# One core: the parts of the first MLP product gathered in three PSUM banks instead of seven

## The chip, the cores and the metric

The kernel runs on one core of a Trainium2 chip. The metric is the device time of one execution in microseconds (us). Three executions of the kernel before took 1241.55, 1241.81 and 1246.07 us; the median is 1241.81 us.

## The reference

A block of 2 x 3008 tokens of width 256 goes through a Fourier transform along the sequence, a complex mixing of the channels with a soft threshold, and the inverse transform. The 6016 tokens that result go through two gated MLPs, one after the other:

```
h = x @ w_in            # 6016 x 256 times 256 x 2048
g = h * sigmoid(1.702 * h)   # in the second MLP: sigmoid(h)
x = g @ w_out           # 6016 x 2048 times 2048 x 256
```

The weights arrive in float64, and the kernel converts them to float32 on the chip.

## The kernel before

The program has four parts: the forward transform, the mixing, the inverse transform, and the two MLPs (layers 0 and 1). The change touches the MLPs alone.

The MLPs run over blocks of 1024 tokens, cut in two halves of 512 (the last block of a layer has halves of 448). Within a block they run over eight pairs of blocks of the inner width, so that there are 2 x 6 x 8 = 96 groups; `group` (L760) issues one. A group multiplies a 2 x 2 matrix of weight blocks with a 2 x 2 matrix of token blocks by the Strassen-Winograd scheme, with seven products in place of eight. `prod` (L767) makes one product of three matmuls (high part of the weights with the high and the low part of the tokens, then the low part of the weights with the high part of the tokens), and each product has a PSUM bank of its own, out of four (`ps0`). The four results are sums of the seven products:

```
h(0,0) = p1 + p2
h(0,1) = p1 + p6 + p5 + p3
h(1,0) = p1 + p6 + p7 + p4
h(1,1) = p1 + p6 + p7 + p5
```

The kernel before forms them in SBUF: ScalarE copies p1 (L794), and VectorE makes seven additions (`add`, L784), each of an SBUF tile and a product in PSUM. The tiles are the columns of `yt` that the block itself came from; `order` turns them by one step from group to group.

`gate` (L775) then applies the activation on ScalarE (L776, in place), copies the result to its high part on ScalarE (L778), and subtracts for the low part (L780; mostly on GpSimd, at some places on VectorE). `out_next` issues the second product of an earlier gate: six matmuls (L744), which add up over the whole block in four other banks (`ps1`). When a block is done, VectorE and ScalarE copy the four banks to `yt` (L748).

`hook` hangs other work between the steps: the splits of the next block's seven token factors in a high part (ScalarE, L99) and a low part (L100), the sums for them (L684 to L697), and the conversion of the weights: a DMA of float64 words (L146), one ScalarE instruction (L155), five on VectorE for a block of weights (L160 to L164), an addition (L221), a store (L224). In layer 0's last block the weights of layer 1 are loaded and put in place (L195 to L200, L99, L100). `add` also pumps the VectorE steps that wait in the list `fill`: the list `left` says among how many additions they are spread.

What sets the order: the program is written once, and a scheduler lays out each engine's queue. In some parts the order of the program is kept for VectorE and SyncE (`rest0`, `last0`: VectorE and SyncE; `rest1`, `last1`: VectorE). Each engine runs its own queue in order, and an instruction waits until what it reads is there and what it overwrites has been read; a product's first matmul waits for the last reader of its bank.

## Time and profile before

| | us |
|---|---|
| median of three runs | 1241.81 |
| span of the profiled execution | 1241.9 |
| TensorE matmuls, busy | 1193.9 (96%) |
| VectorE, busy | 904.3 (73%) |
| ScalarE, busy | 709.1 (57%) |
| GpSimd, busy | 691.3 (56%) |
| the additions L784, busy | 450.9 in 672 instructions |
| TensorE idle before the products L772 | 15.2 |

The page lists no time for the profiled execution beside its span; the span is 0.1 us from the median of the runs, so that time and span can be taken as the same here. The MLPs' first matmul starts at 216.4 us, so that they are some 1025 us of the span. Busy times of engines overlap and don't add up to the span. A matmul's duration in the profile (some 394 ns for 512 columns) overlaps with the next one's; the distance from one to the next is what a stretch's length gives when it is divided by their number.

### The profile page before, as it was taken

To read this page: it belongs to the slowest core of one execution; us is meant where nothing else is said; L and a number is where in the kernel's file an instruction comes from. 1 tells how busy PE (TensorE), PEld (TensorE's weight loads), DVE (VectorE), ACT (ScalarE), POOL (GpSimd) and SP (SyncE) were. 2 spreads that over 40 slices of the span, in tenths; PEclk is the share of its full clock that TensorE was granted. 3 is DMA by queue.
4 is the path that set the end of the run, shared out by engine and by line. 5 is a ranking of instruction groups with operands and counts; after the bars stand their busy time and mean duration, and the time that the engine had idled before them with its cause. 6 is when DMAs were issued, how large, how long until landed. Compare 5 with 4: busy or idle time off the path is not lost.

```text
span 1241.9 us, 15776 instructions
## 1 busy us (share of the span) xinstructions
PE 1193.9 (96%) x5220; PEld 969.5 (78%) x5220; DVE 904.3 (73%) x1543; ACT 709.1 (57%) x1393; POOL 691.3 (56%) x579
## 2 busy tenths in 40 slices
PE   7889889799999999999999999999999999999998
PEld 4877679577688787787888977888888888888897
DVE  7899999999967868678758886465564564655654
ACT  3566644656655656556556675565564555554654
POOL 4666655646545647547556575464464554553643
PEclk9889889799999999999999999999999999999999
DMA  8441123111110111111100110000000000000000
GB/s 330 170 160 55 52 73 130 36 52 60 33 44 27 39 39 39 39 39 38 43 18 9 56 39 9 1 35 1 1 34 1 1 35 1 27 8 1 35 1 30
DMA packets 33012, 57.11 MB, mean 46 GB/s; under 512 B 3233, under 2 KB 22689, under 8 KB 31650
## 3 DMA queue, kind: packets, MB, share of 16 engines
q1 hardware_dynamic: 30882, 41.42, 10.3%
q0 software_dynamic: 2048, 14.68, 3.2%
q8 instruction: 41, 0.67, 0.2%
q14 instruction: 41, 0.34, 0.1%
HBM read 44.68 MB, written 11.40 MB: 45 GB/s over the span
## 4 chain that ended last, share of the span: by engine, by line
PE 65%; DVE 7%; issue 2%; ACT 1%; POOL 0%; DMA 0%; DVEq 0%; ACTq 0%
PE o L744 35%; PE x L772 30%; DVE yt L784 3%; DVE cv_s L196 1%; DVE tmp L697 1%; DVE g L780 0%; DVE x L100 0%; ACT yt L776 0%; DMA raw<-in_wo 0%; DVE tmp L691 0%; ACT g L778 0%; ACT wi L99 0%; DVE cv_c L164 0%; ACT x L99 0%; DVE wi L100 0%
## 5 line engine op out<-in xcount | busy, mean ns | idle before, releaser
L784 DVE TENSOR_TENSOR yt<-yt,x 128x512 f32<-128x512 f32 (+1 forms) x672 | 450.9, 673 | 275.2 <-PE x L772 204.8
L780 POOL TENSOR_TENSOR g<-yt,g 128x512 fp32r<-128x512 f32 (+1 forms) x324 | 416.4, 1295 | 418.1 <-ACT g L778 301.2
L744 PE MATMUL o<-g,wo 128*128 128x512 f32 (+1 forms) x2304 | 604.3, 392 | 2.4 <-ACT yt L748 1.1
L772 PE MATMUL x<-x,wi 128*128 128x512 f32 (+1 forms) x2016 | 543.3, 394 | 15.2 <-DVE yt L784 10.8
L744 PEld LDWEIGHTS o<-g,wo 128*128 128x128 f32 x2304 | 432.9, 188 | 101.7 <-ACT g L778 2.8
L772 PEld LDWEIGHTS x<-x,wi 128*128 128x128 f32 x2016 | 378.4, 189 | 108.3 <-DVE yt L784 19.6
L776 ACT ACTIVATE yt<-yt 128x512 f32<-128x512 f32 (+1 forms) x384 | 237.4, 622 | 292.0 <-DVE yt L784 290.0
L778 ACT CAST g<-yt 128x512 fp32r<-128x512 f32 (+1 forms) x384 | 231.9, 609 | 8.6
L780 DVE TENSOR_TENSOR g<-yt,g 128x512 fp32r<-128x512 f32 (+1 forms) x60 | 49.0, 819 | 33.1 <-ACT g L778 33.1
L100 POOL TENSOR_TENSOR x<-yt,x 128x512 fp32r<-128x512 f32 (+1 forms) x41 | 58.5, 1435 | 14.5 <-ACT x L99 12.7
L155 ACT ACTIVATE cv_c<-raw 128x256 f32<-128x256 f32 x64 | 27.8, 438 | 65.6 <-DMA raw<-in_wo 36.6
L794 ACT COPY yt<-x 128x512 f32<-128x512 f32 (+1 forms) x96 | 54.9, 572 | 9.9 <-PE x L772 9.5
L221 POOL TENSOR_TENSOR cv_a<-cv_a,cv_c 128x256 f32<-128x256 f32 x48 | 41.2, 863 | 23.9 <-DVE cv_c L164 21.4
L164 DVE SCALAR_TENSOR_TENSOR cv_c<-raw,cv_c 128x256 f32<-128x256 uint32 x64 | 51.0, 805 | 0.0
L356 PE MATMUL psi<-m,fh 128*128 128x376 f32 (+3 forms) x208 | 48.7, 324 | 0.3 <-ACT rt L623 0.3
L496 PE MATMUL psm<-wc_hi,xtl 128*128 128x512 f32 x96 | 39.3, 413 | 3.3 <-DVE xtl L100 3.3
L356 PE MATMUL psf<-m,xh 128*128 128x376 f32 (+1 forms) x160 | 39.3, 341 | 2.0 <-ACT xh L307 1.2
L496 PE MATMUL psm<-wc_hi,xth 128*128 128x512 f32 x96 | 40.2, 419 | 1.0 <-ACT xth L99 1.0
L356 PE MATMUL psi<-m,fl 128*128 128x376 f32 (+3 forms) x104 | 34.2, 329 | 6.8 <-POOL fl L100 5.0
L496 PE MATMUL psm<-wc_lo,xth 128*128 128x512 f32 x96 | 39.0, 406 | 0.0
L356 PEld LDWEIGHTS psi<-m,fh 128*128 128x128 f32 x208 | 37.1, 196 | 0.5 <-ACT rt L623 0.4
L356 PEld LDWEIGHTS psf<-m,xh 128*128 128x128 f32 x160 | 30.3, 216 | 3.3 <-ACT xh L307 1.7
(111 smaller groups left out, 979.6 us busy)
## 6 DMA issues: line engine op xcount, KB each, us to landing
raw<-in_wi SPq DMA_DIRECT2D x32, 256.0 KB, 2.7
raw<-in_wo SPq DMA_DIRECT2D x32, 256.0 KB, 2.7
raw<-in_x SPq DMA_DIRECT2D x12, 512.0 KB, 4.9
out_t<-yt SPq DMA_DIRECT2D x20, 256.0 KB, 2.0
m<-in_mf POOLq DMA_DIRECT2D x4, 1128.0 KB, 7.9
m<-in_mi POOLq DMA_DIRECT2D x4, 1128.0 KB, 6.2
w_out<-cv_a SPq DMA_DIRECT2D x24, 128.0 KB, 1.7
cv_ld<-w_out SPq DMA_DIRECT2D x24, 128.0 KB, 2.0
```

Of the source, the lines that this page charges most:

```text
L100: (lo_eng or nc.vector).tensor_sub(lo, src, r32(hi))
L164: lambda: stt(out=c, in0=w[:, :, 0], scalar=2.0**-52, in1=c, op0=ALU.mult, op1=ALU.mult),
L221: E('cva', u[2]).tensor_add(a, a, c)
L356: nc.tensor.matmul(ps, a, z, start=i == 0 and x == 0, stop=i == last and x == 2)
L496: nc.tensor.matmul(t, a, w, start=(n == 0), stop=(n == 11 and grp == 1))
L744: nc.tensor.matmul(acc[h, mm], st, mv, start=first and k == 0, stop=last and k == 2)
L772: nc.tensor.matmul(ps, st, mv, start=m == 0, stop=m == 2)
L776: nc.scalar.activation(g, g, func)
L778: nc.scalar.copy(gh, g)
L780: E('gl3' if l else 'gl0' if i == 0 else 'gl2' if i == last else 'gl', ng[0]).tensor_sub(gl, g, r32(gh))
L784: (nc.vector.tensor_sub if sub else nc.vector.tensor_add)(out, u, v)
L794: nc.scalar.copy(ya, p1)
```

## The change

A group still makes the same seven products of 21 matmuls and the same 24 matmuls of the second product. But the products are gathered in three banks X, Z and Y. p1 goes to X, and then p6, p7 and p4 are added to X by TensorE itself (their first matmul no longer has `start`); p5 goes to Z, and p3 is added to it; p2 goes to Y. Between the steps the banks are read: X after p1 and after p6 (copies by ScalarE), after p7 (an addition on VectorE), after p4 (by the activation of the gate itself); Z after p5 (a copy by ScalarE) and after p3 (an addition); Y after p2 (an addition). There are three VectorE additions a group where there were seven, and three ScalarE copies where there was one. The places in `yt` are the same in each group, the order of the gates and of `out_next` is another, and the steps in `fill` are spread over two additions after the hook that makes them, where it was six. Comments were taken out elsewhere, which moves line numbers: L776, L778, L780 and L784 are L775, L777, L779 and L783 in the changed kernel, and L794 is L792, L800 and L803.

```diff
-        def prod(s, k):
-            ps = bank(0, "x")[:, :n]
+        def prod(ps, s, k, first=True):
...
-                nc.tensor.matmul(ps, st, mv, start=m == 0, stop=m == 2)
-            return ps
+                nc.tensor.matmul(ps, st, mv, start=first and m == 0, stop=m == 2, skip_group_check=True)
 
-        def gate(row, h, g):
-            nc.scalar.activation(g, g, func)
+        def gate(row, h, g, src=None):
+            nc.scalar.activation(g, g if src is None else src, func)
...
-        left = [1, 2, 3, 4, 5, 6, 1]
-        p1 = prod(0, 0)
-        nc.scalar.copy(ya, p1)
-        p2 = prod(1, 1)
-        add(yb, ya, p2)
+        left = [1, 2, 1]
+
+        X, Z, Y = (bank(0, "x")[:, :n] for _ in range(3))
+        prod(X, 0, 0)
+        nc.scalar.copy(y1, X)
+        prod(Y, 1, 1)
+        add(y1, y1, Y)
         hook(1)
         if begun:
             out_next()
-        p5 = prod(3, 2)
-        p6 = prod(4, 3)
-        add(ya, ya, p6)
-        gate(0, 0, yb)
+        gate(0, 0, y1)
+        prod(Z, 3, 2)
+        nc.scalar.copy(y2, Z)
+        prod(X, 4, 3, False)
         hook(2)
-        add(yc, ya, p5)
+        nc.scalar.copy(y3, X)
         hook(3)
         if begun:
             out_next()
-        p7 = prod(5, 4)
-        add(ya, ya, p7)
-        add(yd, ya, p5)
+            out_next()
+        prod(X, 5, 4, False)
+        add(y2, y2, X)
         hook(4)
-        if begun:
-            out_next()
-        gate(1, 1, yd)
-        p4 = prod(2, 5)
-        p3 = prod(6, 6)
-        add(ya, ya, p4)
-        add(yc, yc, p3)
-        gate(1, 0, ya)
+        gate(1, 1, y2)
+        prod(Z, 6, 6, False)
         out_next()
+        add(y3, y3, Z)
         hook(5)
-        gate(0, 1, yc)
+        prod(X, 2, 5, False)
+        gate(0, 1, y3)
+        gate(1, 0, y4, X)
```

Three places show how the queues move. The first is a group of layer 0's third block (its seventh pair, `wi6`) on TensorE and on VectorE. TensorE's queue before, from p7 (`x_4748`) to p4 (`x_4770`), each in a bank of its own; `o..` are the banks of the second product, `g_...` gated parts:

```order
L772 MATMUL x_4748<-x_4136,wi6_2814 128x512
L772 MATMUL x_4748<-x_4137,wi6_2814 128x512
L772 MATMUL x_4748<-x_4136,wi6_2814 128x512
L744 MATMUL o00_4222<-g_4688,wo_2686 128x512
L744 MATMUL o00_4222<-g_4687,wo_2686 128x512
L744 MATMUL o01_4226<-g_4688,wo_2686 128x512
L744 MATMUL o01_4226<-g_4687,wo_2686 128x512
L772 MATMUL x_4770<-x_4188,wi6_2814 128x512
L772 MATMUL x_4770<-x_4189,wi6_2814 128x512
L772 MATMUL x_4770<-x_4188,wi6_2814 128x512
```

The same group in the changed kernel, where p7 and p4 go to the same bank X (`x_4572`), and `x_4662` is the next group's X:

```order
L772 MATMUL x_4572<-x_4041,wi6_2795 128x512
L772 MATMUL x_4572<-x_4042,wi6_2795 128x512
L772 MATMUL x_4572<-x_4041,wi6_2795 128x512
L772 MATMUL x_4662<-x_4010,wi7_3009 128x512
L772 MATMUL x_4662<-x_4011,wi7_3009 128x512
L772 MATMUL x_4662<-x_4010,wi7_3009 128x512
L772 MATMUL x_4572<-x_4097,wi6_2795 128x512
L772 MATMUL x_4572<-x_4098,wi6_2795 128x512
L772 MATMUL x_4572<-x_4097,wi6_2795 128x512
```

On VectorE there stood, before, the additions for this group (`x_4723` is p5) one by one between the conversion of a weight:

```order
L784 TENSOR_TENSOR yt_1699<-yt_1699,x_4723 128x512
L160 TENSOR_SCALAR cv_c_4737<-cv_c_4737 128x256
L784 TENSOR_TENSOR yt_1699<-yt_1699,x_4748 128x512
L161 TENSOR_SCALAR cv_c_4737<-cv_c_4737 128x256
L784 TENSOR_TENSOR yt_1699<-yt_1699,x_4723 128x512
L162 SCALAR_TENSOR_TENSOR cv_a_4738<-raw64_4702,cv_c_4737 128x256
L685 TENSOR_TENSOR yt_1699<-yt_1699 128x512
L784 TENSOR_TENSOR yt_1699<-yt_1699,x_4770 128x512
```

Now the addition of p7 stands behind that of another bank (`x_4574`, Y) and a subtraction that waits for ScalarE's cast:

```order
L163 TENSOR_SCALAR cv_c_4517<-cv_a_4518 128x256
L164 SCALAR_TENSOR_TENSOR cv_c_4517<-raw64_4483,cv_c_4517 128x256
L783 TENSOR_TENSOR yt_1699<-yt_1699,x_4574 128x512
L779 TENSOR_TENSOR g_4594<-yt_1699,g_4593 128x512
L783 TENSOR_TENSOR yt_1699<-yt_1699,x_4572 128x512
L160 TENSOR_SCALAR cv_c_4604<-cv_c_4604 128x256
```

Before, p4 could start whether or not p7 had been read; now its first matmul has to wait until VectorE has read X, and only three matmuls lie in between. Over the 96 groups the queue leaves these distances between the steps on X, in matmuls: from p1 to p6 9 to 57 (median 31), from p6 to p7 6 to 39 (median 29), from p7 to p4 three in four groups, five to seven in 14, and nine to 33 (mostly 13) in the other 78. On Z, from p5 to p3, it is 6 to 37.

The second place is ScalarE's queue in layer 0's third block (the weights of layer 1 are converted there). Before, the instruction that waits for a DMA (`cv_c<-raw64`) stands between two gates:

```order
L778 CAST g_4268<-yt_1699 128x512
L155 ACTIVATE cv_c_4365<-raw64_4330 128x256
L776 ACTIVATE yt_1699<-yt_1699 128x512
L778 CAST g_4298<-yt_1699 128x512
L776 ACTIVATE yt_1699<-yt_1699 128x512 x2
L778 CAST g_4315<-yt_1699 128x512
L794 COPY yt_1699<-x_4332 128x512
```

In the changed kernel it stands ahead of the copy of the next group's X (`x_4311`):

```order
L800 COPY yt_1699<-x_4225 128x512
L777 CAST g_4245<-yt_1699 128x512
L803 COPY yt_1699<-x_4224 128x512
L155 ACTIVATE cv_c_4343<-raw64_4309 128x256
L792 COPY yt_1699<-x_4311 128x512
L775 ACTIVATE yt_1699<-yt_1699 128x512
L777 CAST g_4280<-yt_1699 128x512
```

Two copies have come in (L800 and L803), and the copies for which TensorE's next step on X waits now stand behind the conversion.

The third place is the end of TensorE's queue. Before, four `out_next`, 24 matmuls, stand behind the last product:

```order
L772 MATMUL x<-x,wi_7353 128x448 x3
L744 MATMUL o_10863<-g,wo 128x448
L744 MATMUL o_10867<-g,wo 128x448
L744 MATMUL o_10863<-g,wo 128x448 x2
L744 MATMUL o_10867<-g,wo 128x448 x2
L744 MATMUL o_10886<-g,wo 128x448
L744 MATMUL o_10890<-g,wo 128x448
```

Now (`o_10353` and `o_10357` of the second half, `o_10320` and `o_10324` of the first) ten `o` matmuls lie between p7 and p4, and 18 behind p4:

```order
L772 MATMUL x<-x,wi_7064 128x448 x6
L744 MATMUL o_10320<-g,wo 128x448 x2
L744 MATMUL o_10324<-g,wo 128x448 x2
L744 MATMUL o_10320<-g,wo 128x448
L744 MATMUL o_10324<-g,wo 128x448
L744 MATMUL o_10320<-g,wo 128x448 x2
L744 MATMUL o_10324<-g,wo 128x448 x2
L772 MATMUL x<-x,wi_7064 128x448 x3
L744 MATMUL o_10353<-g,wo 128x448
L744 MATMUL o_10357<-g,wo 128x448
L744 MATMUL o_10353<-g,wo 128x448 x2
L744 MATMUL o_10357<-g,wo 128x448 x2
```

The first of these 18 need the gate of h(1,1), which starts when p7 has been added.

## Rows read from the trace of the kernel before

**Rows 1.** The first part of the page: busy time, share of the span and number of instructions of each engine.

```profile
PE 1193.9 (96%) x5220; PEld 969.5 (78%) x5220; DVE 904.3 (73%) x1543; ACT 709.1 (57%) x1393; POOL 691.3 (56%) x579
```

**Rows 2.** Busy time of each engine in stretches of the MLPs. A row has the stretch and its length, then TensorE, its weight load, VectorE, ScalarE and GpSimd with the number of instructions, then the granted TensorE clock, the share of the DMA engines and GB/s.

```profile
212.00:255.00 43.00, 36.13 (x141) 27.97 (x140) 42.46 (x78) 25.28 (x53) 27.40 (x27) 0.84 0.14 43
255.00:340.00 85.00, 80.98 (x334) 61.32 (x334) 81.95 (x157) 53.73 (x105) 45.36 (x40) 1.00 0.15 46
400.00:660.00 260.00, 257.88 (x1095) 204.40 (x1094) 190.51 (x316) 151.51 (x270) 150.48 (x121) 1.00 0.12 35
660.00:760.00 100.00, 95.44 (x433) 81.37 (x433) 84.07 (x150) 67.69 (x150) 65.26 (x57) 0.98 0.12 35
760.00:1190.00 430.00, 430.00 (x1860) 348.77 (x1859) 241.44 (x345) 237.65 (x416) 223.35 (x174) 1.00 0.04 13
850.00:900.00 50.00, 50.00 (x216) 40.21 (x215) 24.42 (x36) 26.09 (x45) 21.61 (x17) 1.00 0.00 0
```

**Rows 3.** Groups of instructions over the whole program: line, engine, operation, out<-in, count, busy us and mean ns of one, then the idle time of the engine before them and who ended it.

```profile
L744 PE MATMUL o<-g,wo 128*128 128x512 f32 (+1 forms) x2304 | 604.3, 392 | 2.4 <-ACT yt L748 1.1 <-DVE g L780 0.7 <-ACT g L778 0.4
L772 PE MATMUL x<-x,wi 128*128 128x512 f32 (+1 forms) x2016 | 543.3, 394 | 15.2 <-DVE yt L784 10.8 <-ACT yt L794 3.5 <-DVE x L100 0.7
L784 DVE TENSOR_TENSOR yt<-yt,x 128x512 f32<-128x512 f32 (+1 forms) x672 | 450.9, 673 | 275.2 <-PE x L772 204.8 <-ACT yt L794 36.0 <-POOL g L780 12.9
...
L780 POOL TENSOR_TENSOR g<-yt,g 128x512 fp32r<-128x512 f32 (+1 forms) x324 | 416.4, 1295 | 418.1 <-ACT g L778 301.2 <-issue 67.9 <-PE x L772 39.0
...
L776 ACT ACTIVATE yt<-yt 128x512 f32<-128x512 f32 (+1 forms) x384 | 237.4, 622 | 292.0 <-DVE yt L784 290.0
L778 ACT CAST g<-yt 128x512 fp32r<-128x512 f32 (+1 forms) x384 | 231.9, 609 | 8.6
...
L794 ACT COPY yt<-x 128x512 f32<-128x512 f32 (+1 forms) x96 | 54.9, 572 | 9.9 <-PE x L772 9.5
```

**Rows 4.** TensorE's queue at the start of the MLPs: start, length, what, and in brackets how long TensorE had been idle and who ended that.

```profile
216.40 2.95 PE L772 MATMUL x<-x,wi 128*128 128x512 f32 x12
222.72 1.65 PE L772 MATMUL x<-x,wi 128*128 128x512 f32 x3 [3.36 <-ACT yt L794]
225.63 1.65 PE L772 MATMUL x<-x,wi 128*128 128x512 f32 x3 [1.26 <-DVE yt L784]
227.08 1.09 PE L744 MATMUL o<-g,wo 128*128 128x512 f32 x2
230.40 3.25 PE L772 MATMUL x<-x,wi 128*128 128x512 f32 x6 [2.24 <-DVE yt L784]
```

**Rows 5.** What VectorE does just before the third of these waits ends, in the same form.

```profile
226.89 2.86 DVE L666 TENSOR_TENSOR yt<-rt 128x376 f32<-128x376 f32 x2
229.68 0.68 DVE L784 TENSOR_TENSOR yt<-yt,x 128x512 f32<-128x512 f32 x1
```

**Rows 6.** Who TensorE waits for, in the stretch 255 to 345 us and in the stretch 680 to 780 us: us in total, times, longest.

```profile
PE x L772 <- DVE yt L784: 3.4, 4, 2.0
PE o L744 <- DVE g L780: 0.5, 2, 0.4
...
PE x L772 <- DVE yt L784: 3.5, 4, 1.8
PE x L772 <- DVE x L100: 0.7, 1, 0.7
PE o L744 <- ACT g L778: 0.2, 1, 0.2
```

**Rows 7.** TensorE's queue where layer 0 ends and layer 1 begins.

```profile
747.40 1.36 PE L772 MATMUL x<-x,wi 128*128 128x512 f32 x3 [1.84 <-DVE yt L784]
748.55 1.91 PE L744 MATMUL o<-g,wo 128*128 128x512 f32 x4
```

**Rows 8.** Who ScalarE waits for in the stretch 400 to 660 us (the conversion of layer 1's weights), the row of the weights of the second product: us in total, times, longest.

```profile
ACT cv_c L155 <- DMA raw<-in_wo: 26.8, 16, 2.6
```

**Rows 9.** ScalarE's groups of instructions in the same stretch, in the form of rows 3.

```profile
L776 ACT ACTIVATE yt<-yt 128x512 f32<-128x512 f32 x97 | 61.0, 631 | 63.3 <-DVE yt L784 63.0
...
L155 ACT ACTIVATE cv_c<-raw 128x256 f32<-128x256 f32 x20 | 8.7, 437 | 33.1 <-DMA raw<-in_wo 26.8 <-DMA raw<-in_wi 6.3
```

**Rows 10.** ScalarE's queue around one such wait, and SyncE's issue of the DMA that ends it.

```profile
535.62 0.43 ACT L155 ACTIVATE cv_c<-raw 128x256 f32<-128x256 f32 x1 [2.31 <-DMA raw<-in_wo]
536.68 0.63 ACT L776 ACTIVATE yt<-yt 128x512 f32<-128x512 f32 x1 [0.62 <-DVE yt L784]
...
532.82 0.38 SPq L146 DMA_DIRECT2D raw<-in_wo  x1
```

**Rows 11.** The end: TensorE's last matmuls, and the ScalarE, GpSimd and VectorE steps of a gate with 448 columns.

```profile
1232.67 5.09 PE L744 MATMUL o<-g,wo 128*128 128x448 f32 x24
...
1226.85 0.58 ACT L776 ACTIVATE yt<-yt 128x448 f32<-128x448 f32 x1 [0.32 <-DVE yt L784]
1227.46 0.57 ACT L778 CAST g<-yt 128x448 fp32r<-128x448 f32 x1
1228.16 1.15 POOL L780 TENSOR_TENSOR g<-yt,g 128x448 fp32r<-128x448 f32 x1 [0.22 <-POOL g L780]
1232.87 0.62 DVE L784 TENSOR_TENSOR yt<-yt,x 128x448 f32<-128x448 f32 x1 [1.21 <-PE x L772]
```

More of the change, by code (lines that the diff above doesn't have):

```diff
@@ L781, in gate, with add @@
             pend.append((l, i, p, row, h, gh, gl))
-        def add(out, u, v, sub=False):
-            (nc.vector.tensor_sub if sub else nc.vector.tensor_add)(out, u, v)
+        def add(out, u, ps):
+            nc.vector.tensor_add(out, u, ps)
             pump(-(-len(fill) // max(left.pop(), 1)))
-        if p == 0:
-            order[:] = [0, 2, 1, 3]
-        ya, yb, yc, yd = (y[k // 2][k % 2] for k in order)
-        order[:] = [order[1], order[3], order[0], order[2]]
+        (y1, y2), (y3, y4) = y
         begun = (l, i, p) != (0, 0, 0)
-        left = [1, 2, 3, 4, 5, 6, 1]
-        p1 = prod(0, 0)
-        nc.scalar.copy(ya, p1)
-        p2 = prod(1, 1)
-        add(yb, ya, p2)
+        left = [1, 2, 1]
[4 more added lines that the diff above has]
+        add(y1, y1, Y)
         hook(1)
@@ L808, in group @@
             out_next()
-        p7 = prod(5, 4)
-        add(ya, ya, p7)
-        add(yd, ya, p5)
+            out_next()
+        prod(X, 5, 4, False)
+        add(y2, y2, X)
         hook(4)
-        if begun:
-            out_next()
-        gate(1, 1, yd)
-        p4 = prod(2, 5)
-        p3 = prod(6, 6)
-        add(ya, ya, p4)
-        add(yc, yc, p3)
-        gate(1, 0, ya)
+        gate(1, 1, y2)
+        prod(Z, 6, 6, False)
         out_next()
+        add(y3, y3, Z)
         hook(5)
-        gate(0, 1, yc)
-    order = [0, 1, 2, 3]
+        prod(X, 2, 5, False)
+        gate(0, 1, y3)
+        gate(1, 0, y4, X)
     last = len(blocks) - 1
```

## The prediction, made before the changed kernel had run

> **What bounds the kernel now.** I read the page's engine shares first, then the busy time by stretch, then the queue rows where TensorE is not full. TensorE's matmuls are busy for 96% of the span, VectorE 73%, ScalarE 57%, GpSimd 56% [rows 1]. By stretch the picture is sharper [rows 2]: in 760 to 1190 us TensorE has no idle time at all, and 216 matmuls in the 50 us from 850 are 231 ns each. A group's 45 matmuls (21 and 24) so take 10.4 us. The change leaves those 45 as they are. Where TensorE is full it can only do harm; it can help where TensorE waits, and that is little: 15.2 us before the products (10.8 of it for the additions, 3.5 for the copy of p1, 0.7 for a split) and 2.4 us before the second product [rows 3], 17.6 us of 1025.
>
> These waits lie at the start of the MLPs [rows 4], in 255 to 345 us (3.4 + 0.5) and in 680 to 780 us (3.5 + 0.7 + 0.2) [rows 6], and in crumbs that come to 2.1 us over 400 to 660 us, most of layer 0 (260 less 257.88) [rows 2]. In two of the stretches VectorE has no room: 42.46 of 43 us and 81.95 of 85 us busy [rows 2].
>
> **The change part by part.**
>
> *Four additions fewer on VectorE, two copies more on ScalarE.* An addition takes 0.673 us, a copy 0.572 [rows 3]. VectorE loses 4 x 0.673 = 2.7 us a group, 384 x 0.673 = 258 us in all, and falls from 904 to about 646 us. ScalarE gains 2 x 0.572 = 1.14 us a group, 110 us in all, to about 819 us (66%). Per group ScalarE then has 3 copies, 4 activations of 0.622 and 4 casts of 0.609 us [rows 3]: 6.6 of 10.4 us. Beside a full TensorE both numbers are worth nothing.
>
> *Start, 216 to 232 us.* The first wait, 3.36 us for the copy of p1 [rows 4], stays: the copy stands behind the same work. The other two, 1.26 and 2.24 us, are VectorE's; the third is an addition behind two L666 of the inverse transform, 2.86 us [rows 5], which remain. Between p1 and p6 the new order has nine matmuls for TensorE here, between p6 and p7 six. Bounds 0 and -3.5; I take -1, nearer to zero since the L666 rows decide.
>
> *255 to 340 us.* VectorE needs 81.95 us of 85 for 7.4 groups (334 matmuls of 45 each). Without 7.4 x 2.7 = 20 us it has room, and the 3.4 + 0.5 us for L784 and L780 [rows 6] can go. Bounds 0 and -3.9; I take -3.3, since an occasional late split (L100) will keep some.
>
> *The rest of layer 0, 400 to 660 us.* TensorE is idle for 2.1 us [rows 2]. Bounds 0 and -2.1; I take -1.
>
> *The switch to layer 1, 680 to 780 us.* 4.4 us of waits [rows 6], the longest before a p matmul at 747.4 [rows 7], and a granted clock of 0.98 over 660 to 760 us [rows 2], that is about 2 us more, since TensorE worked after this wait at the lower of its two levels (1.2 in place of 2.4 GHz) for a moment: the four matmuls at 748.55 take 1.91 us [rows 7], where two of the same kind took 1.09 and 24 at full clock 5.09 [rows 4, 11]. VectorE has 84 of 100 us there and loses some 9.6 groups x 2.7 = 26. Bounds 0 and -6.4; I take -4. What is late next is the weights' splits on VectorE and GpSimd, which the change does not touch.
>
> *Full stretches.* Nothing to win. What can be lost are new waits on bank X, which is read three times between its four steps. The chain is: last matmul ends, reader starts, reader ends, next step. An addition starts 0.2 us after the matmul behind the one it waits for (1232.87 against 1232.67 [rows 11]), takes 0.67, and a released matmul follows 0.04 us after its end (230.36 against 230.40 [rows 4, 5]): 0.91 us, four matmuls' time. From p1 to p6 and from p6 to p7 there are 29 to 31 matmuls between in the median, 7 us, for a copy of 0.57. From p7 to p4 there are 13 in most groups, 3.0 us. In four groups there are three, 0.69 us: a wait of 0.22 us if VectorE is free, and 0.9 if the subtraction ahead of the addition (0.69 us by that of an addition's size) is still running. Four times that is 0.9 to 3.6 us; the 14 groups with five to seven matmuls (1.16 us or more) have 0.25 us to spare and a conversion step ahead of the addition can take it. Bounds 0 and +8 (18 groups x 0.45); I take +2.
>
> By the Trainium skill ("PSUM — Partial Sum Buffer", section "PSUM bank collisions raise a hardware error") a bank is not shared out by the hardware: a read that meets a matmul in the same bank is an error, so that semaphores have to keep them apart, and the advice is to aim at a different bank while matmuls run. No trace here shows such an error; the order that it forces is the chain above. That speaks against one bank read three times: with nothing in between, 3 x 0.91 us in 96 groups would be 262 us. The trace of before has only such waits as come to 14.3 us, with a bank for each product [rows 3]; by the distances above, nearly all of the 262 is covered, and the sum keeps its +2.
>
> *ScalarE's copies behind the conversion.* In 400 to 660 us the instruction L155 waits 20 times for a DMA, 26.8 + 6.3 us [rows 9], at most 2.6 [rows 8]; in one place 2.31, and the gate behind it waits 0.62 more [rows 10]. Now the copy of X may stand behind it. The 7 us between p1 and p6 cover 2.6 + 0.44 + 0.57 = 3.6 us. I take 0 here, and keep what it costs if ScalarE has no room for the second rival.
>
> *The end.* Before, 24 `o` matmuls ran behind the last product in 5.09 us without a break [rows 11]. Now 18 do, and ten lie between p7 and p4. The first of the 18 need g(1,1), which comes p7 + addition 0.62 + activation 0.58 + cast 0.57 (+ GpSimd 1.15 for the low part) [rows 11] = 1.8 to 2.9 us later; ten `o` and three p4 matmuls are 13 x 0.206 = 2.7 us. The last gate, h(1,0), starts only after p4: 0.58 + 0.57 + 1.15 = 2.3 us, against 12 `o` of the gates before it, 2.5 us. Bounds 0 and +2.5; I take +1.
>
> *Sum.* -1 - 3.3 - 1 - 4 + 2 + 1 = -6.3 us. The profiled execution's span is 1241.9 us, 0.1 from the median of 1241.81: 1235.5 us.
>
> **Rivals.**
>
> *First: the waits change hands.* TensorE's waits of 17.6 us are of the stages where splits, conversions and L666 crowd, and these remain on VectorE; ScalarE's copies and GpSimd's low parts (1.3 us each, 691 us [rows 1, 3]) end last in place of the additions. For it: GpSimd already ends 12.9 us of VectorE's waits [rows 3]. Against it: VectorE is the one without slack in 255 to 340. Time: the -9.3 of the first four terms shrinks to -3, with the +3 of the others: 1242 (1239 to 1245). Chance 0.18.
>
> *Second, slower: ScalarE's queue fills in layer 0.* In 400 to 660 us ScalarE is busy for 151.5 of 260 us [rows 2]; in the rest, 108.5 us, its queue is held: 63.3 us by gates that wait for an addition, 33.1 us by L155 that waits for a DMA [rows 9]. The change adds 2 x 25 copies of 0.572, 28.6 us, to these 25 groups (97 activations, four a group): 151.5 + 28.6 + 108.5 = 289 us, if the holds stay as they are, in a stretch where TensorE needs 258. Before, a late ScalarE delayed only gates that are used a group later; now it holds X itself, and so TensorE. It decides from the point at which the holds fall by less than 289 - 260 = 29 us. Against it: a gate that comes later finds its addition done and waits less, and two additions ahead of a gate are gone. Price: if they fall by 15, half of that, 14 us: 1235.5 + 14 = 1249.5. Chance 0.20.
>
> *Third: all of VectorE's waits vanish.* Then -17.6 + 3.4 (the first wait) - 2 (clock) + 2 for X and the end: 1228. For it: VectorE loses 29% of its work; against it: [rows 5]. Chance 0.12.
>
> That the change doesn't do what it says could only be so in counts: 288 additions and 288 copies must be there; I give it nothing.
>
> **How the numbers follow.** The forecast, 1231 to 1240 us, has 0.50. What a measurement of this kernel tells from no change is about 0.5%, 6.2 us: faster is below 1235.6. Of the forecast 0.31 lies below, 0.19 above; with the third rival faster has 0.43, with the first "same" has 0.37, the second is slower, 0.20. The range takes in most of the third and the centre of the second: 1226 to 1252.
>
> **What would show it.** Right: 288 additions on L783 and 288 copies; TensorE still without idle time in 760 to 1190 us; VectorE's share in 255 to 340 well under 85%, and its waits there under 1 us; the wait of some 3.4 us at the start still there; a gap of about 1 us among the last 18 matmuls. Wrong: TensorE waiting in most groups for the copies on ScalarE or for the addition of p7, matmuls that come more than 233 ns apart in 850 to 900 us, or 255 to 340 and 680 to 780 us that keep their waits under another engine's name.

## The result and the profile after

The changed kernel takes 1259.3 us (1258.1 to 1260.5, four runs) against 1243.8 us (1241.6 to 1246.1, four runs) beside it: a ratio of 1.0126, with a 95% interval of 1.0108 to 1.0145. It is 15.5 us slower; 1235.5 was forecast, and the range ended at 1252. The profiled execution has a span of 1256.4 us, 14.5 over that of before.

The change does what it says. The first part of the page of the changed kernel, in the form of [rows 1]:

```profile
PE 1194.6 (95%) x5220; PEld 960.0 (76%) x5220; DVE 662.7 (53%) x1159; ACT 790.4 (63%) x1585; POOL 692.2 (55%) x579
```

VectorE has 384 instructions and 242 us less to do, ScalarE 192 and 81 us more, and TensorE the same 5220 matmuls. The groups of instructions, in the form of [rows 3]:

```profile
L744 PE MATMUL o<-g,wo 128*128 128x512 f32 (+1 forms) x2304 | 600.8, 392 | 11.0 <-ACT g L777 4.5 <-POOL g L779 4.3 <-DVE g L779 1.7
L772 PE MATMUL x<-x,wi 128*128 128x512 f32 (+1 forms) x2016 | 536.1, 393 | 16.6 <-DVE yt L783 8.5 <-ACT yt L800 4.4 <-ACT yt L792 2.6
...
L783 DVE TENSOR_TENSOR yt<-yt,x 128x512 f32<-128x512 f32 (+1 forms) x288 | 188.3, 672 | 420.9 <-PE x L772 392.9 <-ACT yt L792 22.8 <-ACT cv_c L155 4.6
```

TensorE's waits rose from 17.6 to 27.6 us. Those for an addition fell little, from 10.8 to 8.5, while VectorE now idles 421 us before the additions. New are waits for gates, in the second product 10.5 of its 11.0 us in place of 1.1 of 2.4, and for the copy of Z (L800), 4.4. The idle time grew by 10.0 us and the MLPs, as the pieces below show, by 13.8: a matmul's record lasts 394 ns where the next matmul starts some 233 ns behind it, so that the first 0.16 us of a wait doesn't show as idle time. The stretches of [rows 2]:

```profile
212.00:255.00 43.00, 34.40 (x132) 24.79 (x133) 38.65 (x73) 26.10 (x58) 28.20 (x26) 0.92 0.15 43
255.00:340.00 85.00, 80.39 (x333) 61.16 (x332) 63.41 (x121) 58.14 (x115) 42.24 (x37) 1.00 0.15 44
400.00:660.00 260.00, 254.66 (x1069) 197.71 (x1068) 133.71 (x221) 169.54 (x310) 147.43 (x118) 1.00 0.12 36
660.00:760.00 100.00, 93.93 (x439) 81.22 (x437) 58.08 (x108) 74.08 (x167) 65.52 (x56) 1.00 0.11 34
760.00:1190.00 430.00, 428.20 (x1835) 343.74 (x1836) 131.32 (x183) 271.96 (x498) 225.44 (x174) 1.00 0.04 13
850.00:900.00 50.00, 50.00 (x216) 40.23 (x215) 11.01 (x16) 28.11 (x50) 20.97 (x18) 1.00 0.00 1
```

In 850 to 900 us there are 216 matmuls, as before: a group inside a block takes the same time in both kernels. In 255 to 340 us VectorE went from 82 to 63 of 85 us, and TensorE made one matmul less.

One thing in these rows helps the changed kernel. In 212 to 255 us the granted clock was 0.92, before 0.84 [rows 2]: TensorE worked for less of this stretch at the lower of its two levels (1.2 in place of 2.4 GHz). By these shares that is 0.08 x 43 = 3.4 us of work at full clock (an estimate), which hide as much of the first block's loss. It isn't shown to come from the change: a later run with nearly the same TensorE queue (the gates one later, below) has 0.96 in this stretch, and 0.98 in 660 to 760 us, as before, where the changed kernel has 1.00.

For a finer reading I take from each trace the start of the first of the MLPs' 4320 matmuls and of every 45th behind it: 96 pieces, each a group's worth of work. In both kernels a piece of plain groups takes 10.50 us (after, a few in layer 0 up to 10.62); 21 of the 96 pieces differ by more than 0.3 us. Put together (the pieces from 0, 8, 40, 50 and 95; the last column is from the last matmul's start to the end of the span):

| us | MLPs to end of span | first block | blocks 2 to 5 of layer 0 | last block of layer 0, first 2 groups of layer 1 | rest of layer 1 | last group | end |
|---|---|---|---|---|---|---|---|
| before | 1025.5 | 103.3 | 340.8 | 104.2 | 463.7 | 9.0 | 4.5 |
| after | 1039.3 | 105.3 | 348.7 | 103.6 | 466.9 | 9.8 | 4.9 |

The MLPs are 13.8 us longer: +2.0 in the first block, +7.9 in layer 0's middle, -0.6 at the switch (where layer 0 ends and layer 1 begins), +3.3 in layer 1, +1.2 at the end; the other 0.7 of the span stands ahead of them. The 7.9 come in steps: the last but one piece of a block is 12.5 us long, three times (from 385, 474 and 562 us), and the first of the next block 12.6 to 12.7, where before had 10.5 and 11.5 to 12.8. TensorE's queue at the first of these places, in the form of [rows 4]:

```profile
388.10 1.81 PE L744 MATMUL o<-g,wo 128*128 128x512 f32 x6
390.39 2.60 PE L744 MATMUL o<-g,wo 128*128 128x512 f32 x10 [0.48 <-POOL g L779]
392.83 2.60 PE L772 MATMUL x<-x,wi 128*128 128x512 f32 x9
395.79 0.72 PE L744 MATMUL o<-g,wo 128*128 128x512 f32 x2 [0.35 <-ACT g L777]
...
412.18 1.56 PE L772 MATMUL x<-x,wi 128*128 128x512 f32 x6
414.58 0.96 PE L772 MATMUL x<-x,wi 128*128 128x512 f32 x3 [0.85 <-ACT yt L800]
```

ScalarE's queue ahead of the last of them: casts of the next block's factors (L99), a copy of X (L803), a gate and a copy of a bank of the second product (L748) stand back to back before the copy of Z:

```profile
411.41 0.62 ACT L99 CAST x<-tmp 128x512 fp32r<-128x512 f32 x1 [1.57 <-DVE tmp L697]
411.94 0.58 ACT L803 COPY yt<-x 128x512 f32<-128x512 f32 x1
412.42 0.63 ACT L775 ACTIVATE yt<-yt 128x512 f32<-128x512 f32 x1
412.95 0.61 ACT L99 CAST x<-yt 128x512 fp32r<-128x512 f32 x1
413.46 0.59 ACT L748 COPY yt<-o 128x512 f32<-128x512 f32 x1
413.94 0.60 ACT L800 COPY yt<-x 128x512 f32<-128x512 f32 x1
```

This last wait is no loss by itself: its piece takes 12.69 us and took 12.77 before. The 2.0 us are lost in the piece ahead of it, by the wait for GpSimd at 390.39 and by one chain. The queue has three matmuls between p7 and p4, and p4 needs the addition of p7; so does a gate whose `o` matmuls come three matmuls later. The addition ends at 394.42, p4 starts at 394.47, 0.25 us late, and the `o` matmuls wait for the gate's cast until 395.79, 0.5 us late:

```profile
393.73 0.69 DVE L783 TENSOR_TENSOR yt<-yt,x 128x512 f32<-128x512 f32 x1 [4.54 <-PE x L772]
```

```profile
394.45 0.63 ACT L775 ACTIVATE yt<-yt 128x512 f32<-128x512 f32 x1 [3.82 <-DVE yt L783]
395.12 0.62 ACT L777 CAST g<-yt 128x512 fp32r<-128x512 f32 x1
```

Where the layers meet there are three waits of 2 us:

```profile
736.25 1.59 PE L772 MATMUL x<-x,wi 128*128 128x448 f32 x6 [1.93 <-DVE yt L783]
...
756.26 1.69 PE L772 MATMUL x<-x,wi 128*128 128x512 f32 x6 [1.91 <-ACT yt L800]
757.79 0.63 PE L744 MATMUL o<-g,wo 128*128 128x512 f32 x2
760.41 1.66 PE L772 MATMUL x<-x,wi 128*128 128x512 f32 x6 [2.00 <-DVE yt L783]
```

The second is for a copy of Z. On ScalarE it stands behind a load of an activation table of 1.28 us, and a gate, a copy and a cast after that:

```profile
753.08 1.28 ACT L775 ACT_TABLE_LOAD   x1
```

At the third, VectorE's queue shows a batch of weight steps ahead of the addition that TensorE waits for:

```profile
756.85 1.09 DVE L195 TENSOR_TENSOR cv_s<-cv_ld 128x128 f32<-128x128 f32 x1
757.86 1.36 DVE L196 TENSOR_TENSOR cv_s<-cv_ld 128x128 f32<-128x128 f32 x1
759.14 0.41 DVE L100 TENSOR_TENSOR wi<-cv_ld,wi 128x256 fp32r<-128x256 f32 x1
759.48 0.28 DVE L198 TENSOR_TENSOR cv_s<-cv_s,cv_ld 128x128 f32<-128x128 f32 x1
759.68 0.68 DVE L783 TENSOR_TENSOR yt<-yt,x 128x512 f32<-128x512 f32 x1
```

### The profile page after: what moved, and what is told of

It is laid out like the page before. It is cut to its first block, busy times and chain, and to the rows that moved or that the text cites. A ratio compares the mean times of both kernels' runs of the same rounds, so it can differ in the third digit from the quotient of the medians.

```text
span 1256.4 us, 15169 instructions
## 1 busy us (share of the span) xinstructions
PE 1194.6 (95%) x5220; PEld 960.0 (76%) x5220; DVE 662.7 (53%) x1159; ACT 790.4 (63%) x1585; POOL 692.2 (55%) x579
## 4 chain that ended last, share of the span: by engine, by line
PE 68%; DVE 18%; ACT 5%; POOL 4%; issue 3%; DMA 1%; SPq 0%; DVEq 0%; POOLq 0%; ACTq 0%
PE o L744 35%; PE x L772 30%; DVE yt L783 2%; ACT yt L775 1%; PE psf L353 1%; POOL g L779 1%; DVE fl L100 1%; DVE x L100 1%; PE psf L356 1%; ACT g L777 1%; DVE f L535 1%; DVE cv_a L162 1%; DVE yt L666 1%; DVE th L519 1%; DVE cv_c L163 1%
## 5 line engine op out<-in xcount | busy, mean ns | idle before, releaser
L779 POOL TENSOR_TENSOR g<-yt,g 128x512 fp32r<-128x512 f32 (+1 forms) x324 | 417.9, 1305 | 391.5 <-ACT g L777 288.1
L744 PE MATMUL o<-g,wo 128*128 128x512 f32 (+1 forms) x2304 | 600.8, 392 | 11.0 <-ACT g L777 4.5
L772 PE MATMUL x<-x,wi 128*128 128x512 f32 (+1 forms) x2016 | 536.1, 393 | 16.6 <-DVE yt L783 8.5
L744 PEld LDWEIGHTS o<-g,wo 128*128 128x128 f32 x2304 | 429.2, 188 | 117.9 <-ACT g L777 11.3
L772 PEld LDWEIGHTS x<-x,wi 128*128 128x128 f32 x2016 | 376.1, 188 | 111.4 <-DVE yt L783 16.5
L783 DVE TENSOR_TENSOR yt<-yt,x 128x512 f32<-128x512 f32 (+1 forms) x288 | 188.3, 672 | 420.9 <-PE x L772 392.9
L775 ACT ACTIVATE yt<-yt 128x512 f32<-128x512 f32 (+1 forms) x288 | 177.2, 623 | 191.9 <-DVE yt L783 191.6
L777 ACT CAST g<-yt 128x512 fp32r<-128x512 f32 (+1 forms) x384 | 229.3, 608 | 3.0
L779 DVE TENSOR_TENSOR g<-yt,g 128x512 fp32r<-128x512 f32 (+1 forms) x60 | 52.9, 883 | 117.9 <-ACT g L777 94.1
L792 ACT COPY yt<-x 128x512 f32<-128x512 f32 (+1 forms) x96 | 55.3, 577 | 69.1 <-POOL g L779 50.9
L775 ACT ACTIVATE yt<-x 128x512 f32<-128x512 f32 (+1 forms) x96 | 56.3, 587 | 16.9 <-PE x L772 16.1
L800 ACT COPY yt<-x 128x512 f32<-128x512 f32 (+1 forms) x96 | 55.3, 576 | 9.7 <-PE x L772 4.5
L803 ACT COPY yt<-x 128x512 f32<-128x512 f32 (+1 forms) x96 | 55.5, 578 | 8.4 <-POOL g L779 4.2
L155 ACT ACTIVATE cv_c<-raw 128x256 f32<-128x256 f32 x64 | 28.0, 439 | 41.2 <-DMA raw<-in_wo 22.0
L163 DVE TENSOR_SCALAR cv_c<-cv_a 128x256 uint32<-128x256 uint32 x64 | 48.9, 767 | 0.2
```

Source lines behind the costliest of these rows:

```text
L163: lambda: ts(cu, au, 0xFF800000, None, op0=band),
L744: nc.tensor.matmul(acc[h, mm], st, mv, start=first and k == 0, stop=last and k == 2)
L772: nc.tensor.matmul(ps, st, mv, start=first and m == 0, stop=m == 2, skip_group_check=True)
L775: nc.scalar.activation(g, g if src is None else src, func)
L777: nc.scalar.copy(gh, g)
L779: E('gl3' if l else 'gl0' if i == 0 else 'gl2' if i == last else 'gl', ng[0]).tensor_sub(gl, g, r32(gh))
```

## The experiments

Three theories stood at the start. S: ScalarE, with two copies more a group, is late at the block changes. G: the gathering itself costs, by the round trips on X and Z, whoever reads them. O: the new order of steps, gates and `out_next`, or the queue made of it, costs. Later runs split O into the order and TensorE's queue. Each run below is the changed kernel with the edit shown, if nothing else is said. The part ahead of the MLPs ends between 215.8 and 222.7 us in these profiles, though TensorE's queue there is the same, so that I compare the length of the MLPs beside the time.

**The order and the gathering apart.** The kernel of the first run has the new order with seven banks, that is, as before, one taken anew for each product out of the same four, and seven additions; its places in `yt` were a mistake, since p1's copy goes to the place that the group before frees last, and in a block's first group over tokens that are still to be read, so that this group computes something else:

```diff
-        nc.scalar.copy(y1, X)
...
+        nc.scalar.copy(y4, p1)
...
+        add(y4, y4, p6)
...
+        add(y3, y4, p5)
...
+        add(y2, y4, p5)
```

> The order of the steps, gates and out_next of the changed kernel, but seven banks and seven VectorE additions a group as before. If the new order is what costs: about as the changed kernel, 10 to 16 us over before, with the same 2 us waits at the ends of layer 0's blocks. If the gathering in banks (the copies on ScalarE, or the waits on X) costs: within 3 us of before, and the groups at the block ends at about 10.5 us.

1383.9 us, ratio 1.114 (1.110 to 1.118). It tells nothing of the order; beside the mended form, which differs in the places alone, it shows what such places cost, 127 us. The mended form turns the places from group to group:

```diff
+        ya, yb, yc, yd = (y[k // 2][k % 2] for k in order)
+        order[:] = [order[1], order[3], order[2], order[0]]
...
+        nc.scalar.copy(ya, p1)
```

> Mended form of the order run: the steps, gates and out_next in the new order, seven banks and seven additions as before, and the places in yt turned from group to group as before, so that p1's copy goes where the gate was done first. If the order of steps by itself costs: 8 to 16 us over before. If it is the gathering in banks that costs: within 3 us of before.

1257.3 us, 1.0104 (1.0068 to 1.0141); MLPs 1037.3. As O says: with the additions and banks of before, the new order alone is 11.8 us longer in the MLPs, close to the 13.8 of the changed kernel. The places differ: its plain groups and layer 0's block ends are at 10.50, and it loses where blocks begin and the layers meet (107.6). The other corner has the gathering in the order of before:

```diff
-        gate(0, 0, y1)
...
+        nc.scalar.copy(y3, X)
+        gate(0, 0, y1)
...
+        prod(X, 2, 5, False)
         prod(Z, 6, 6, False)
+        add(y3, y3, Z)
+        gate(1, 0, y4, X)
         out_next()
-        add(y3, y3, Z)
...
-        prod(X, 2, 5, False)
...
-        gate(1, 0, y4, X)
```

> Gathered in X, Z and Y as in the changed kernel, but p6, p7, p4, p3, the gates and out_next in the order of before. If the order costs: within 3 us of before. If the gathering costs: 10 to 16 us over before. In between, if each has a part.

1293.4 us, 1.0398 (1.0371 to 1.0425); MLPs 1074.4. Neither expectation: in layer 0 every other plain group takes 11.5 us, and in the MLPs TensorE waits 19.2 us for gates and 17.3 for additions and copies out of the banks (in the changed kernel 10.5 and 15.5). So the two parts don't add up. The gathering is 34 us better in the new order than in the old one, and the new order costs about as much with seven banks.

**Less for ScalarE (S).**

```diff
-        nc.scalar.copy(y2, Z)
+        nc.vector.tensor_copy(y2, Z)
...
-        nc.scalar.copy(y3, X)
+        nc.vector.tensor_copy(y3, X)
```

> The changed kernel with the copies of Z after p5 and of X after p6 on VectorE in place of ScalarE, so that ScalarE has as many instructions as before and VectorE five reads of a bank a group. If ScalarE's extra 1.14 us a group is what delays the steps: 6 to 12 us faster than the changed kernel, 1247 to 1253. If the round trips on the banks cost, whichever engine reads them: within 2 us of the changed kernel, or slower.

1286.3 us, 1.0346 (1.0307 to 1.0385).

```diff
-                (nc.scalar.copy if mm else nc.vector.tensor_copy)(y, acc[h, mm])
+                nc.vector.tensor_copy(y, acc[h, mm])
```

> The changed kernel with all four copies of the second product's banks at a block's end (L748) on VectorE; two of them were on ScalarE. If ScalarE's queue at the block changes is what TensorE waits for: the wait for the copy L800 (0.85 us) and the one behind it (0.3 us) go at each change, 3 to 6 us in all. If not: within 1 us of the changed kernel.

1262.7 us, 1.0152 (1.0127 to 1.0176): 3.4 us more than the changed kernel; the pieces where layer 0's blocks begin take 13.8 us in place of 12.7.

```diff
-        split(hi, lo, src, lo_eng=E('xl1' if l else 'xl0' if i == 0 else 'xl', k))
+        split(hi, lo, src, hi_eng=nc.vector.tensor_copy, lo_eng=E('xl1' if l else 'xl0' if i == 0 else 'xl', k))
```

> The changed kernel with the casts of the next block's seven token factors (L99, x<-yt and x<-tmp) on VectorE, seven a block. If bursts on ScalarE at the block changes make gates and copies late: the groups at the ends of layer 0's blocks, 12.5 and 12.7 us, come down by 0.5 to 1.5 us each, 4 to 8 us in all. If the additions on VectorE are what is late there: no gain, 0 to 4 us slower.

1284.5 us, 1.0320 (1.0273 to 1.0367).

```diff
-        split(hi, lo, src, lo_eng=E('xl1' if l else 'xl0' if i == 0 else 'xl', k))
+        split(hi, lo, src, hi_eng=nc.vector.tensor_copy, lo_eng=E('xl1' if l else 'xl0' if i == 0 else 'xl', k))
...
-'xl': 'PPVVPPP', 'xl0': 'PVVVPPP', 'xl1': 'PPPVVPP'
+'xl': 'VVVVVVV', 'xl0': 'VVVVVVV', 'xl1': 'VVVVVVV'
```

> As the run before it, and the low parts of these factors (L100), most of which GpSimd makes, on VectorE too. If GpSimd is late at the block ends because the factors stand ahead of the gates' low parts: the waits for L779 of GpSimd (0.48 us a block end) go, and the group of 12.5 us falls by a further 0.5 us; if not, as the run before it or slower.

1274.9 us, 1.0242 (1.0207 to 1.0277). (The last two lines are entries of the kernel's table `CFG`, as in the edits below.) All four take work from ScalarE or GpSimd, give it to a VectorE that is idle half of the time, and are slower. With the copies on VectorE every other plain group of layer 0 takes 12.2 us: VectorE works in program order there, and a copy that waits for TensorE can hold the rest. With the casts moved, the block-end pieces do return from 12.5 to 10.5 us, but the pieces beside them grow by more (17.3 us at worst). S has the places right. That it has the cause wrong these runs don't show by themselves, since they lengthen a queue of VectorE for which TensorE waits too; that the same work takes less time in another order of TensorE's queue (below) does show it for the larger part of the loss.

**The batches on VectorE.**

```diff
-        left = [1, 2, 1]
+        left = [2, 3, 1]
```

> The changed kernel with the steps in fill spread over the three additions that follow the hook, not two. If the additions that TensorE's next step on X or Z waits for are late because batches of weight steps stand ahead of them on VectorE: the waits of 1.93 and 2.00 us where the layers meet shrink by 0.5 to 1 us each, and the total by 1 to 4 us. If VectorE's order plays no part: within 1 us.

1259.7 us, 1.0118 (1.0087 to 1.0149). No gain. Here too the block-end piece returns to 10.50, and the next two take 0.8 and about 2.3 us more than in the changed kernel. Three different edits move the wait from one piece to the next; that spoke for the queue as a whole, and not for one late instruction.

**The gates' distance and TensorE's queue (O).**

```diff
         prod(Z, 6, 6, False)
-        out_next()
+        if begun:
+            out_next()
```

> The changed kernel with the second product one gate further behind: the first group issues no out_next, so that each gate has some 11 matmuls (2.6 us) more before its o matmuls. If what costs is that the gates, which now come in a bunch behind p7, p3 and p4, are late for their o matmuls: TensorE's waits before L744 (11.0 us) nearly vanish, the 12.5 us groups at layer 0's block ends return to 10.5, and the MLPs become 6 to 10 us shorter. If the steps on X, Z and Y are what is late: L744's waits fall but L772's 16.6 us stay or grow, and the MLPs change by less than 3 us.

1261.6 us, 1.0151 (1.0130 to 1.0171). The numbers are those of the second expectation (9.9 us of waits before L744, 17.3 before L772, MLPs 0.6 us longer), but it was hardly tested: matmuls of the first and of the second product follow each other in TensorE's queue as in the changed kernel at all but 90 of 4320 places, and piece by piece the times are nearly those of the changed kernel (12.51 against 12.49 at the block end). It seems that the scheduler put the `o` matmuls back where it had them, wherever `out_next` stands in the program.

```diff
-'rest0': 'DVE,SP', 'rest1': 'DVE', 'last0': 'DVE,SP', 'last1': 'DVE'
+'rest0': 'DVE,SP,PE', 'rest1': 'DVE,PE', 'last0': 'DVE,SP,PE', 'last1': 'DVE,PE'
```

> The changed kernel with TensorE's queue in the order of the program behind the first block: between the steps on X there are then 12, 12 and 9 matmuls in every group, where the scheduler's queue has 27 to 57, 6 to 39 and 3 to 33. If round trips on X through a busy ScalarE and VectorE are what costs: slower than the changed kernel, by 10 us or more, since 12 matmuls (2.8 us) cover less than 29. If the scheduler's uneven queue is what costs (steps that stand three to seven matmuls apart, gates that are used too soon): faster by 5 us or more.

1272.2 us, 1.0235 (1.0218 to 1.0253). The groups of TensorE's matmuls tell which part is late:

```profile
L744 PE MATMUL o<-g,wo 128*128 128x512 f32 (+1 forms) x2304 | 588.0, 394 | 22.4 <-POOL g L779 15.9 <-DVE g L779 3.4 <-ACT g L777 2.6
L772 PE MATMUL x<-x,wi 128*128 128x512 f32 (+1 forms) x2016 | 515.6, 393 | 16.5 <-DVE yt L783 6.2 <-ACT yt L800 5.6 <-ACT yt L792 2.0
```

Distances of 12, 12 and 9 matmuls on X cover the round trips (16.5 us of waits, as with 29 and 13), but the second product waits 22.4 us, 21.9 of it for gates. Both edits together:

> Both of the two runs before it. If the steps on the banks are covered by 12, 12 and 9 matmuls and only the gates are late, 1245 or less; if the round trips cost, not below the changed kernel.

1248.8 us, 1.0046 (1.0031 to 1.0061); MLPs 1030.6. The same two groups:

```profile
L744 PE MATMUL o<-g,wo 128*128 128x512 f32 (+1 forms) x2304 | 579.6, 393 | 6.0 <-ACT g L777 2.5 <-POOL g L779 2.1 <-DVE g L779 1.2
L772 PE MATMUL x<-x,wi 128*128 128x512 f32 (+1 forms) x2016 | 516.9, 394 | 15.5 <-DVE yt L783 5.0 <-ACT yt L792 2.5 <-ACT yt L800 2.4
```

The second product's waits fell from 22.4 to 6.0 us and the time by 23 us, with the same work on every engine (VectorE is busy for 670.5 us in place of 672.4, ScalarE for 785.0 in place of 787.5). Of the changed kernel's 13.8 us in the MLPs 8.6 are gone, 2.5 of layer 1's 3.3 among them (464.5), although the granted clock in 212 to 255 us is that of before again (0.84).

**The same queue for the others.** In each of these TensorE works in program order behind the first block, gates one later. The new order with seven banks:

> The new order of steps with seven banks and seven additions, and with TensorE's queue in program order and the gates one later, as in the best run so far. If the gathering in three banks costs by itself, this is faster than that run (1248.8), by 3 us or more, about 1244. If the gathering is worth something once the queue is right, it is slower, 1250 or more. Within 2 us: gathering as such is neutral.

1262.5 us, 1.0156 (1.0139 to 1.0174), slower, as the second expectation has it; TensorE waits 14.5 us for the additions there. The kernel before:

> The kernel before with TensorE's queue in program order and the gates one later. If the scheduler's queue fits the kernel before and only the new steps need another one: the kernel before gets slower, by 2 us or more. If that queue is better for any kernel: faster than before by 2 us or more.

1249.2 us, 1.0051 (1.0035 to 1.0068), 6.7 us more than the kernel before took beside it (1242.5). The gathering in the order of before:

> Gathered in three banks, the steps in the order of before, TensorE's queue in program order, gates one later. Between the steps on X stand 12, 6 and 6 matmuls, 2.8, 1.4 and 1.4 us, against 0.9 us for a round trip. If the round trip alone counts: within 3 us of the best run, 1248.8. If a reader that is busy with other work makes it longer: TensorE waits before L772 in the plain groups of layer 0, and it is 5 us or more slower.

1282.0 us, 1.0319 (1.0302 to 1.0336). The three rows of its timeline show what was the second rival's mechanism, TensorE first and then ScalarE:

```profile
442.73 0.97 PE L772 MATMUL x<-x,wi 128*128 128x512 f32 x3 [0.59 <-ACT yt L801]
```

```profile
440.13 0.59 ACT L799 COPY yt<-x 128x512 f32<-128x512 f32 x1
441.76 0.43 ACT L155 ACTIVATE cv_c<-raw 128x256 f32<-128x256 f32 x1 [1.05 <-DMA raw<-in_wi]
442.10 0.57 ACT L801 COPY yt<-x 128x512 f32<-128x512 f32 x1
```

ScalarE waits 1.05 us for a DMA, and the copy of X behind it (L801) lets TensorE wait 0.59 us, since p6 and p7 have only six matmuls between them. TensorE waits for this copy 25 times, 17.1 us in all; 17 times (11.1 us) the copy stands right behind an L155 that had waited 0.7 to 2.6 us itself. With 12 matmuls between, in the run of 1248.8 us, TensorE waits for the copy in its place (L803) four times, 1.2 us.

With one queue for all, then: before 1249.2, gathered 1248.8, seven banks in the new order 1262.5, gathered in the old order 1282.0. With the scheduler's: 1243.8, 1259.3, 1257.3, 1293.4. Gathering against before is nothing (0.4 us) by the first and 15.5 us by the second; and within the new order gathering is worth 13.7 us in the first queue, and nothing in the second. The kernel before was tried in this one plain queue alone, not in program order without the later gates.

**What is left of the loss.** Each run here is that of 1248.8 us with the edit shown. TensorE in program order from the first block on:

```diff
-'mlp': 'none'
+'mlp': 'PE'
```

> The gathering kernel with TensorE's queue in program order from the first block on, gates one later. If in the first block too it is the scheduler's queue that makes steps on X and gates late: the 2.7 us that its first block still lies over before go, 1246 or less. If there the weights' conversion on VectorE and ScalarE bounds: no change or slower.

1250.4 us, 1.0061 (1.0043 to 1.0079); the first block 107.4 us, against 105.2 in the run that it changes and 103.3 before (so that 1.9 us were to be won there, and not 2.7). Program order is not better there. Fill over three additions (the edit of `fill_over_three`):

> The run with program order and gates one later, and fill spread over three additions. If the batches on VectorE are what TensorE still waits for at the block changes (L783 5.0 us, L100 2.2 us): 1 to 3 us faster. If not, within 1 us.

1249.9 us, 1.0051 (1.0033 to 1.0069): 1.1 us more, no gain. VectorE's queue by the scheduler:

```diff
-'rest0': 'DVE,SP,PE', 'rest1': 'DVE,PE', 'last0': 'DVE,SP,PE', 'last1': 'DVE,PE'
+'rest0': 'SP,PE', 'rest1': 'PE', 'last0': 'SP,PE', 'last1': 'PE'
```

> The best run (TensorE in program order behind the first block, gates one later), with VectorE's queue behind the first block laid out by the scheduler in place of program order. If VectorE's order of the program is what makes the last reads of X and the splits late at the block changes: 2 to 5 us faster, near the kernel before. If not: within 1 us, or slower.

1280.5 us, 1.0301 (1.0285 to 1.0316): VectorE's order of the program is worth 32 us, and not what costs. Gates two later:

```diff
         hook(1)
-        if begun:
+        if begun and (l, i, p) != (0, 0, 1):
             out_next()
```

> The best run with the gates two later than in the changed kernel. If gates are still late: the 5.8 us of waits before L744 shrink and it gains 1 to 4 us. If what is left are the steps on the banks and the first block (L772, 15 us): within 1 us.

1248.2 us, 1.0039 (1.0024 to 1.0053); MLPs 1029.2, layer 1 from its third group on 463.7 as before. Within 1 us of one later in time. This is the fastest gathered form; none of the runs is faster than the kernel before.

## Why the prediction was wrong

- *The bound* was right: TensorE's 10.50 us a group stayed, 850 to 900 us has its 216 matmuls, and nothing was won where TensorE was full.
- *Counts and work* were right: 288 additions at 0.672 us; VectorE 663 us (646 forecast), ScalarE 790 (819). The two new copies take 55.3 and 55.5 us, the 110 of the forecast; but the total of an engine counts only once the time in which the records of neighbours overlap (L803 above starts at 411.94, lasts 0.58, and the next instruction starts at 412.42), and ScalarE's rose by 81.
- *Start and 255 to 340 us, -1 and -3.3:* wrong. The wait that was to stay at 3.4 us is 2.0, and the first piece gained 2.5 us; but its waits fell by 1.1 us only (2.02, 0.82, 1.98, 0.59 and 0.34 in place of the 3.36, 1.26 and 2.24 of [rows 4]). The rest goes with the clock (0.92 in place of 0.84), for which the start had no term. The next four pieces lost 9.0: in 237 to 291 us TensorE waits 7.1 us, 5.6 of it for gates, and before it waited 0.8. Then the block's last piece won 4.4 back, and the block ended 2.0 us longer. VectorE got the room (63 of 85 us), and the waits changed hands, as the first rival had it: in 255 to 345 us TensorE waits 0.5 us for an addition in place of 3.4, and 4.0 for gates in place of 0.5 [rows 6]. That is the prediction's own sign of being wrong, a stretch that keeps its waits under another engine's name.

```profile
PE o L744 <- ACT g L777: 2.0, 2, 1.3
PE o L744 <- DVE g L779: 1.2, 3, 0.8
PE o L744 <- POOL g L779: 0.8, 1, 0.8
PE x L772 <- DVE yt L783: 0.5, 1, 0.5
```

- *The rest of layer 0, -1:* this is the step that failed most, +7.9 us over blocks 2 to 5. The sum asked what of TensorE's 2.1 us of idle time would go, and looked for new waits only on X. It left out that a new order of steps makes a new queue for TensorE, with another distance from each gate to its `o` matmuls and from each split to its use, at places where ScalarE, GpSimd and VectorE have the next block's factors on top. In these blocks (322 to 671 us) TensorE waits 3.5 us for gates and 2.5 for copies of Z; before (320 to 660 us) it waited 2.1 us in all, 0.4 of it for gates.
- *The switch, -4:* -0.6. The wait at 747.4 [rows 7] went and three of 2 us came, two for additions (736 and 760 us) and one for a copy of Z (756): in 680 to 780 us TensorE's waits rose from 4.4 to 6.2 us. What was gained all the same goes with the clock (1.00 in place of 0.98 in 660 to 760 us), and that may be luck: with the gates one later, in nearly the same queue, it is 0.98 again, and the switch takes the 104.2 us of before. The working here also read one row wrongly: the two matmuls of 1.09 us ran at the lower level themselves (0.84 in 212 to 255 us [rows 2]); at full clock four take 1.09 us (at 242.22 in the trace of before).
- *Full stretches, +2 for X:* the wait is real and smaller than its term: in layer 0, p4 behind three matmuls waits 0.25 us at 394.5, 482.9 and 571.2 us, the lower of the two sizes worked out. But the stretch is not free: in layer 1 the four block changes cost 0.8 to 1.0 us each, 3.3 in all, which no term held.
- *The copies behind the conversion, 0:* right for the changed kernel, where TensorE waits for no copy of X in 400 to 660 us, and the mechanism was shown where it isn't covered. The second rival had the sign and, at 1249.5, the nearest time. Its sum can't be tested in a stretch of fixed length, where ScalarE's idle time falls by whatever work comes in (108.5 to 90.5 us here). The waits can: those of gates for additions fell from 63.0 to 54.6 us and those of L155 for DMAs from 33.1 to 17.2, 24 of the 29 us that it asked for; TensorE made 26 matmuls less, some 6 us, and ScalarE ended 4.2 of TensorE's 5.2 us of waits there (2.5 for copies of Z, 1.7 for casts of gates). So its account was half right. But taking work from ScalarE made it worse, and the same work in another queue took 4.2 us off layer 0's middle (344.5 against 348.7). So it is not ScalarE's load by itself.
- *The end, +1:* right, 1.2 us, with a wait of 0.52 us for a low part of GpSimd among the last 18 matmuls.

```profile
1247.22 0.57 PE L744 MATMUL o<-g,wo 128*128 128x448 f32 x2
1248.32 3.55 PE L744 MATMUL o<-g,wo 128*128 128x448 f32 x16 [0.52 <-POOL g L779]
```

- *Chances:* slower had 0.20, and the argument for it rested on one engine's sum. That every one of 96 groups gets another order was named in the change and priced nowhere.

What the runs show is this: with one plain queue for both, the gathering in its new order takes the time of the kernel before; the scheduler's queue for the new steps is 10.5 us worse than program order with later gates, while for the kernel before it is 6.7 us better (1242.5 against 1249.2). Of the two edits neither does it alone (1272.2 and 1261.6). What stays open: which single instruction starts the chains at a block's end (three edits moved the wait and none removed it), why the first block lies some 2 us or more over before in every gathered form, and what makes up the 5.6 us by which the gathered form in the better queue is still slower than the kernel before (1248.8 against 1243.2 beside it).

## What to carry to other kernels

Before pricing what an engine is spared, ask what ends TensorE's waits: 242 us less on VectorE bought nothing, because the waits were those of chains (read, gate, cast, low part, second product) at a few places, and the chains' ends moved with the order. When a change gives every group another order, the queue that is made of it is part of the change: compare both forms with the same simple queue as well, and give consumers one step more distance before blaming an engine. An accumulation bank that is read between its steps cost nothing in plain groups (10.50 us) where nine or more matmuls (2.1 us here) lay between, and much with six where a conversion that waited held the reader's queue.

## What was not expected of the hardware

One step of the conversion, L163 (128 x 256, one operand), took 0.767 us on average in the changed kernel and 0.354 before. Sorted by whether GpSimd was inside an instruction 50 ns after its start, the 64 of the changed kernel are 21 of 0.285 us (at most 0.294) and 43 of 1.002; before, 49 of 0.285 and 15 of 0.581. Of the 43, 33 end 0.15 to 0.21 us behind the GpSimd instruction under which they started, as in this pair:

```profile
419.15 1.33 DVE L163 TENSOR_SCALAR cv_c<-cv_a 128x256 uint32<-128x256 uint32 x1
```

```profile
419.04 1.30 POOL L779 TENSOR_TENSOR g<-yt,g 128x512 fp32r<-128x512 f32 x1 [2.03 <-ACT g L777]
```

VectorE's step starts second, lasts for 1.33 us in place of 0.285, and both end within 0.15 us of each other. The Trainium skill ("SBUF — State Buffer", section "Who interferes with whom") says that such a step can take a pair of ports that it shares with GpSimd, and that whoever comes second is blocked for the whole instruction; the rows agree. The new order put more of these steps under a gate's low part on GpSimd, which cost some 26 us (64 x 0.413). But it took another step of the conversion out from under it: L164, also 128 x 256, went from 0.805 to 0.472 us, and the five steps L160 to L164 together from 149.6 to 151.8 us.

```profile
L164 DVE SCALAR_TENSOR_TENSOR cv_c<-raw,cv_c 128x256 f32<-128x256 uint32 x64 | 51.0, 805 | 0.0
...
L163 DVE TENSOR_SCALAR cv_c<-cv_a 128x256 uint32<-128x256 uint32 x64 | 22.3, 354 | 0.0
```

```profile
L163 DVE TENSOR_SCALAR cv_c<-cv_a 128x256 uint32<-128x256 uint32 x64 | 48.9, 767 | 0.2
...
L164 DVE SCALAR_TENSOR_TENSOR cv_c<-raw,cv_c 128x256 f32<-128x256 uint32 x64 | 30.0, 472 | 1.2
```

So the waits for GpSimd moved from one step to another, and VectorE's work hardly changed by them; that is why they aren't in the account above.
